# Ranking the last five steps by their whole chain, and issuing seven of eight stores from GpSimd, in a two-problem attention kernel

## The chip, the cores and the metric

The kernel runs on one core of a Trainium2 chip. The metric is the device time of one execution in microseconds (us), as the median of several runs; lower is better. A profiled execution gives the trace that all rows come from. Its engines are PE (matrix multiply; PEld is its weight load), DVE or VectorE, ACT or ScalarE, POOL or GpSimd, and SP or SyncE, which issues DMA transfers. "SPq" is SyncE's queue of DMA instructions.

## The reference

Two attention blocks over a key/value cache, A (grouped heads: 4 key/value heads for 32 query heads) and B (32 key/value heads), whose results are put side by side:

```python
def _B_ref(x, k_cache, v_cache, wq, wo):      # B, Sq, D = 16, 32, 1024; H, Sk, Dh = 32, 1024, 128
    q = (x @ wq).reshape(B, Sq, H, Dh).transpose(0, 2, 1, 3)
    scores = einsum("bhqd,bhkd->bhqk", q, k_cache) * Dh ** -0.5
    p = softmax(scores, axis=-1)
    o = einsum("bhqk,bhkd->bhqd", p, v_cache)
    return o.transpose(0, 2, 1, 3).reshape(B, Sq, H * Dh) @ wo
# _A_ref is the same with k and v of 4 heads, each repeated for 8 query heads
a = _A_ref(A_x, ...); b = _B_ref(B_x, ...)
return concatenate([a, b], axis=-1)           # 16 x 32 x 2048, bfloat16
```

All inputs are bfloat16. The caches of B alone are 2 x 128 MiB, so each byte is read once and used little.

## The kernel before, in words

The 512 token rows are handled in NG = 4 groups G of 128. Work is cut into quads: 128 B quads (two batches by two heads, each with 1024 keys) and 128 A quads (one batch, four query heads). Step t of the program holds B quad t and, a little ahead, an A quad; "B124" is B quad 124. The function `oproj(pi, blk, G)` multiplies what the quads of a group gave with a block of `wo`; "oA3.3" is A's last block (3) for group 3, "oB7.2" is B's last block (7) for group 2. Block by block the products are added in `acc`; after the last block the group's 128 x 1024 result is stored by one DMA of 256 KB. There are eight such stores, one for each of two problems and four groups.

One B quad goes through these operations, under the lines of the kernel before:

- two K transfers of 512 KB each (`kb_dma`, L772) into two of 8 K slots, and two V transfers of 512 KB each (`vb_dma`, L785) into one of 3 V slots. V of quad t can be issued when quad t - 3 has done its last use of the slot; K of quad t when quad t - 4 has done its scores. Transfers are issued in order by SyncE.
- a transpose of each K half on VectorE (`KBt_tr`, L806), scores on PE into one of two score buffers (`scoresB`, L847, 32 matmuls), the negated maximum on VectorE (`max`, L857), the exponential with its sum on ScalarE (`exp`, L870).
- a transpose of the probabilities on PE (`PT_tr`, L882), its copy out of PSUM (`PT_ev`, L531, by ScalarE or VectorE), the product with V on PE (`PVB`, L912; `PVA`, L904 for A), reciprocal (L921) and normalization (`norm`, L928 or L929), a small transpose (`OT_tr`, L934) and its copy (`OT_ev`, L531).
- after the last quad of a group the projection on PE (L703, two halves of 512 columns), for the last block two sums on VectorE (`accF`, L717), and the store (`out_dma`, L720).

PE's work other than scores goes through four PSUM banks that these operations take and free.

The order on every engine is made by a planner, `list_schedule`, when the program is built. It walks through the operations with assumed durations, and of those that could start within 0.35 us of the earliest it takes the one of highest rank `bl`. The rank is the length of the chain that hangs on an operation, but only through users of the same step or an earlier one (`STEP_NEAR = 0`), less 3 us for each step (`STEP_US`), so that earlier steps go first. What comes out is fixed: each engine runs its list in order and waits by semaphores. A wait of SyncE for an `accF` ahead of a store therefore also holds the transfers listed behind that store. At the end SyncE waits for every transfer's semaphore (L418).

Of the kernel before, what the change touches and what calls it, by code (L numbers as in the profile page):

```python
# [10 lines left out]
BF = mybir.dt.bfloat16  # L11
# [19 lines left out]
LOOK = 0.35  # L31
STEP_US = 3
STEP_NEAR = 0
QB0 = [0, 3, 6, 9]
QA0 = [13 + (i * 9) // 8 for i in range(8)]
QB1 = [24 + (i * 9) // 8 for i in range(8)]
# [25 lines left out]
def dma_time(op):  # L62
    size, us = PACKET.get(op.name, PACKET_DEFAULT)
    return op.dur / size * us / 16
# [48 lines left out]
class Prog:  # L113
# [118 lines left out]
    def list_schedule(self, lat=0.05, look=LOOK):  # L232
        ops = self.ops
        n = len(ops)
        users = [[] for _ in range(n)]
# [6 lines left out]
        def odur(op):  # L242
            if op.dma_key is not None:
                return DMA_FIRST + dma_time(op) + DMA_LAST
            return op.dur[0] + op.dur[1]
        bl = [0.0] * n
        for i in range(n - 1, -1, -1):
            m = 0.0
            for u in users[i]:
                v = bl[u] + lat  # L250
                if v > m and ops[u].step <= ops[i].step + STEP_NEAR:
                    m = v
            bl[i] = odur(ops[i]) + m + ops[i].prio + PRIO_BONUS.get(ops[i].name.split("@")[0], 0.0)
        for i in range(n):
            bl[i] -= STEP_US * ops[i].step
        ready_t = [0.0] * n
        free = {}
        ready = {}
# [182 lines left out]
def build(nc, pa, pb, out):  # L441
    P = 128
    Bn, Sq, D = pa["x"].shape
    NTOK = Bn * Sq
    assert Sq == 32 and Bn % 4 == 0
    NG = NTOK // P
# [21 lines left out]
    out_flat = out.rearrange("b s c -> (b s) c")  # L468
# [3 lines left out]
    cols = [0, D]  # L472

    pr = Prog()
    stack = contextlib.ExitStack()
    with stack:
        def sb(name, shape, dt):
            return stack.enter_context(nc.sbuf_tensor(name, shape, dt))
# [15 lines left out]
        acc = sb("acc", [P, 2, NG, D], F32)  # L494
# [14 lines left out]
        def bank(v):  # L509
            return ps_g[:, v.idx, :]  # L510
# [12 lines left out]
        def evac(dst_ap, src_ap, reads, writes, name, eng=None, wtag=None, rtag=None, mul=None):  # L523
            def emit(e):
                dst = dst_ap() if callable(dst_ap) else dst_ap
                src = src_ap() if callable(src_ap) else src_ap
                if mul is not None:
                    if hasattr(e, "activation"):
                        return e.activation(dst, src, ACTF.Copy, scale=mul)
                    return e.tensor_scalar(dst, src, mul, None, ALU.mult)  # L530
                return e.copy(dst, src) if hasattr(e, "activation") else e.tensor_copy(dst, src)  # L531
            eng = eng or "any"
            pr.add(eng, emit, reads=reads, writes=writes, name=name if eng == "any" else name + "@" + eng, wtag=wtag, rtag=rtag)
# [35 lines left out]
        def lazy_flush(prefix):  # L569
            last = -1  # L570
            for i, (k, _, _) in enumerate(lazy):
                if k[:len(prefix)] == prefix:
                    last = i
            for _ in range(last + 1):
                lazy.pop(0)[1]()
# [113 lines left out]
        def oproj(pi, blk, G):  # L689
            gp = (blk * NG + G) % 2  # L690
            nh = HS if pi == 0 else MS
            nblk = NSB if pi == 0 else NMSB
            OT = OTA_sb if pi == 0 else OTB_sb
            wo_ = woA_sb if pi == 0 else woB_sb
            wo_res = "woA" if pi == 0 else "woB"
            lazy_flush(("wo", pi, blk))
            for oh in range(NOH):
                v = Virt("bank", "pj")
                for h0_ in range(0, nh, 2):
                    def e_op(e, oh=oh, h0_=h0_, v=v):  # L700
                        last = None
                        for hh in range(h0_, h0_ + 2):
                            last = e.matmul(bank(v)[:, 0:OUTW], OT[:, gp, hh, :], wo_[:, hh, oh * OUTW:(oh + 1) * OUTW],  # L703
                                            start=(hh == 0), stop=(hh == nh - 1))
                        return last
                    pr.add("pe", e_op, reads=[("OT", pi, gp, h0_), ("OT", pi, gp, h0_ + 1), (wo_res, h0_), (wo_res, h0_ + 1)], writes=[v],
                           name="oprojA" if pi == 0 else "oprojB",
                           dur=0.45 * OUTW / 512, rtag={(wo_res, h0_): blk, (wo_res, h0_ + 1): blk, ("OTv", pi, gp): (blk, G)})
                a_ap = acc[:, pi, G, oh * OUTW:(oh + 1) * OUTW]
                o_ap = acc[:, pi, G, :].bitcast(BF)[:, oh * OUTW:(oh + 1) * OUTW]  # L710
                if blk == 0:
                    evac(a_ap, lambda v=v: bank(v)[:, 0:OUTW], reads=[], writes=[v, ("acc", pi, G, oh)], name="acc0")
                elif blk < nblk - 1:
                    pr.add("dve", lambda e, a_ap=a_ap, v=v: e.tensor_tensor(a_ap, a_ap, bank(v)[:, 0:OUTW], ALU.add),  # L714
                           reads=[], writes=[v, ("acc", pi, G, oh)], name="acc+")
                else:
                    pr.add("dve", lambda e, a_ap=a_ap, o_ap=o_ap, v=v: e.tensor_tensor(o_ap, a_ap, bank(v)[:, 0:OUTW], ALU.add),  # L717
                           reads=[], writes=[v] + [("acc", pi, G, x) for x in range(oh + 1)], name="accF")
            if blk == nblk - 1:
                pr.add("sp", lambda e: e.dma_start(out_flat[G * P:(G + 1) * P, cols[pi]:cols[pi] + D], acc[:, pi, G, :].bitcast(BF)[:, 0:D]),  # L720
                       reads=[("acc", pi, G, x) for x in range(NOH)], dma_key=f"out{pi}_{G}", name="out_dma", dur=P * D * 2)

        class Quad:
# [320 lines left out]
        def plan(t, f, *a):  # L1044
            q_plan.setdefault(t, []).append(lambda: f(*a))

        PER = 8 * NG
        for G in range(NG):
            plan(QB0[G], qprojB, 1, G)
        for p_ in range(NIT // PER - 1):  # L1050
            at = QB0[-1] if p_ == 0 else (p_ - 1) * PER + (QB1 if p_ == 1 else QB_T)[-1]
            plan(at, wq_load, 0, p_ + 1)
# [13 lines left out]
        def stepA(qA):  # L1066
            tA = qA.t % (NG * 8)
            if qA.t == min(1, NIT - 1):
                for hh in pro_heads:
                    qprojA_head(0, hh)  # L1070
                wo_loadA(0)
            quadA_all(qA)
            if qA.last_of_group:
                oproj(0, qA.s, qA.G)
                if qA.G == NG - 1 and qA.s + 1 < NSB:
                    wo_loadA(qA.s + 1)

        for t in range(NIT):
            cur_step[0] = t
            pr.step = t  # L1080
            qB = quadsB[t]
            tB = t % (NG * 4)
            quadB_all(qB)
            target = min(NIT, -(-(t + 1) * NIT // NAS))
            while ia[0] < target:
                stepA(quadsA[ia[0]])
                ia[0] += 1
            tn = t + (4 - t % 4)
            if tn < NIT:
                qn = quadsB[tn]  # L1090
                if t % 4 == 0:
                    qprepB_tr(qn.m, qn.G)
                    qprepB_sh(qn.m, qn.G)
            for what in q_plan.get(t, ()):
                what()
            if qB.last_of_group:
                oproj(1, qB.m, qB.G)
                if qB.G == NG - 1 and qB.m + 1 < NMSB:
                    wo_loadB(qB.m + 1)
            lazy_pop(LAZY_PER_STEP)  # L1100
# [3 lines left out]
        if SCHED:  # L1104
            pr = pr.list_schedule()
# [41 lines left out]
```

## Time and profile before

| what | value |
|---|---|
| median of 3 runs | 891.7 us (891.68 to 892.2) |
| profiled execution | 894.39 us, of it the span 892.3 us |
| granted PE clock, mean | 0.994 |
| HBM read / written | 337.64 MB / 2.10 MB, 381 GB/s over the span |
| PE, VectorE, ScalarE busy | 92%, 83%, 68% of the span |
| POOL busy | 1.1 us, 8 instructions |
| stores (`out_dram`) | 8 of 256 KB, issued by SyncE, median 8.0 us from issue to landing |

The span runs from the first instruction to the last of the profiled execution; 2.09 us of that execution lie outside it. A row of a window gives the busy time and the number of instructions for each engine. A row of the chain gives its start, its length and what ran. A row of the timeline gives start, length, engine, line and operation. The time from issue to landing of a transfer contains its wait behind others in the queue.

### The profile page before, as it was taken

What the parts mean: (1) busy time and instruction counts of PE and PEld (TensorE: products, weight loads), DVE (VectorE), ACT (ScalarE), POOL (GpSimd) and SP (SyncE); (2) the same over time, 40 slices, a digit from 0 to 9 for tenths busy, and PEclk for the clock granted to TensorE, in tenths of its full rate; (3) what the DMA queues carried; (4) which work ended last, traced back from release to release, by engine and by line L of the source; (5) the groups of instructions that cost most, each with busy time, mean ns of one, the idle gap of its engine ahead of it and who ended that gap; (6) DMA issues with size and microseconds to landing.
All of it is one profiled execution on the core that took longest, in us unless ns stands there. A gap on an engine that the chain in (4) does not pass through costs nothing.

```text
span 892.3 us, 29320 instructions
## 1 busy us (share of the span) xinstructions
PE 820.2 (92%) x12864; PEld 469.4 (53%) x12864; DVE 739.5 (83%) x1030; ACT 608.6 (68%) x1347; POOL 1.1 (0%) x8
## 2 busy tenths in 40 slices
PE   6999899999999999999999999999899878978976
PEld 3365565556555455555555555555456545544543
DVE  0398888879987888889898888898899889888985
ACT  3387886776768577675777677676767767565763
POOL 0000000000000000000000000000000000000000
PEclk9999999999999999999999999999999999998999
DMA  9999999999999999999999999999999999999994
GB/s 318 397 395 392 391 393 396 392 389 395 395 366 387 396 395 390 380 393 395 395 393 394 391 393 394 372 395 394 394 378 380 393 395 395 396 394 382 394 374 166
DMA packets 145278, 341.65 MB, mean 383 GB/s; under 512 B 12032, under 2 KB 12032, under 8 KB 145152
## 3 DMA queue, kind: packets, MB, share of 16 engines
q1 hardware_dynamic: 145152, 339.79, 100.7%
q8 instruction: 101, 1.65, 0.8%
q14 instruction: 25, 0.20, 0.1%
HBM read 337.64 MB, written 2.10 MB: 381 GB/s over the span
## 4 chain that ended last, share of the span: by engine, by line
PE 53%; DMA 18%; DVE 14%; ACT 9%; SPq 3%; issue 1%; DVEq 0%; ACTq 0%
DMA KB_sb<-in_B_k_cache_dram 14%; PE ps_s L847 12%; PE ps_g L703 9%; PE ps_g L882 9%; ACT P_sb L870 6%; DVE stat L857 6%; DVE KB_sb L806 6%; PE ps_g L912 5%; PE ps_g L615 4%; PE ps_g L904 4%; PE ps_s L827 3%; PE ps_g L634 3%; PE ps_g L798 2%; ACT PT_sb L531 2%; SPq L785 2%; DMA VB_sb<-in_B_v_cache_dram 1%
## 5 line engine op out<-in xcount | busy, mean ns | idle before, releaser
L857 DVE TENSOR_REDUCE stat<-ps_s 128x1 f32<-128x1024 f32 x256 | 305.4, 1208 | 53.3 <-PE ps_s L847 43.9
L806 DVE STREAM_TRANSPOSE KB_sb<-KB_sb 128x1024 f32<-128x1024 f32 x256 | 310.2, 1230 | 35.8 <-DMA KB_sb<-in_B_k_cache_dram 32.7
L870 ACT ACTIVATE P_sb<-ps_s,stat 128x1024 bf16<-128x1024 f32 x256 | 286.1, 1119 | 60.9 <-DVE stat L857 59.2
L882 PE MATMUL ps_g<-id,P_sb 128*128 128x128 f32 x1024 | 172.7, 295 | 9.7 <-ACT OTA_sb L531 3.2
L847 PE MATMUL ps_s<-KB_sb,QR 32*32 32x512 bf16 x4096 | 160.1, 397 | 23.1 <-ACT P_sb L870 17.4
L882 PEld LDWEIGHTS ps_g<-id,P_sb 128*128 128x128 f32 x1024 | 149.1, 207 | 48.1 <-issue 9.2
L531 ACT COPY PT_sb<-ps_g 128x512 f32<-128x512 f32 x238 | 138.2, 593 | 50.9 <-PE ps_g L882 49.8
L928 ACT ACTIVATE O_sb<-ps_g,stat 128x128 bf16<-128x128 f32 x186 | 67.9, 371 | 62.9 <-PE ps_g L912 36.5
L912 PE MATMUL ps_g<-VB_sb,PT_sb 128*32 128x128 bf16 x4096 | 92.0, 224 | 7.0 <-ACT PT_sb L531 3.6
L847 PEld LDWEIGHTS ps_s<-KB_sb,QR 32*32 32x32 bf16 x4096 | 47.1, 89 | 85.0 <-ACT P_sb L870 27.0
L827 PE MATMUL ps_s<-KTA_sb,QT_sb 128*128 128x512 bf16 x256 | 87.0, 383 | 4.2 <-ACT P_sb L870 4.1
L912 PEld LDWEIGHTS ps_g<-VB_sb,PT_sb 128*32 128x32 bf16 x4096 | 60.5, 97 | 55.3 <-issue 36.4
L904 PE MATMUL ps_g<-VA_sb,PT_sb 128*128 128x128 bf16 x1024 | 77.6, 220 | 3.1 <-ACT PT_sb L531 1.2
L904 PEld LDWEIGHTS ps_g<-VA_sb,PT_sb 128*128 128x128 bf16 x1024 | 61.0, 98 | 31.6 <-issue 13.9
L634 PE MATMUL ps_g<-wq_sb,xT_sb 128*128 128x512 bf16 x256 | 72.8, 388 | 3.9 <-DMA wq_sb<-in_B_wq_dram 3.9
L703 PE MATMUL ps_g<-woB_sb,OTB_sb 128*128 128x512 bf16 x256 | 67.6, 380 | 3.4 <-ACT PT_sb L531 1.3
L703 PE MATMUL ps_g<-woA_sb,OTA_sb 128*128 128x512 bf16 x256 | 62.5, 380 | 0.8 <-DVE OTA_sb L531 0.3
L934 PE MATMUL ps_g<-ident,O_sb 128*128 128x128 bf16 x256 | 52.5, 223 | 4.5 <-ACT O_sb L928 3.6
L615 PE MATMUL ps_g<-xT_sb,wq_sb 128*128 128x512 bf16 x192 | 55.5, 380 | 0.4 <-ACT QR L531 0.2
L870 ACT ACTIVATION_READ_ACCUMULATOR P_sb<-ps_s,stat 128x1 f32 x256 | 51.6, 202 | 0.0
L531 ACT COPY OTA_sb<-ps_g 128x64 f32<-128x64 f32 x114 | 24.5, 216 | 37.2 <-PE ps_g L934 36.6
L714 DVE TENSOR_TENSOR acc<-acc,ps_g 128x512 f32<-128x512 f32 x64 | 41.0, 675 | 8.7 <-PE ps_g L703 8.4
(42 smaller groups left out, 511.9 us busy)
## 6 DMA issues: line engine op xcount, KB each, us to landing
VB_sb<-in_B_v_cache_dram SPq DMA_DIRECT2D x256, 512.0 KB, 12.2
KB_sb<-in_B_k_cache_dram SPq DMA_DIRECT2D x256, 512.0 KB, 12.4
KA_sb<-in_A_k_cache_dram SPq DMA_DIRECT2D x64, 256.0 KB, 12.3
VA_sb<-in_A_v_cache_dram SPq DMA_DIRECT2D x64, 256.0 KB, 12.2
wq_sb<-in_B_wq_dram SPq DMA_DIRECT2D x16, 512.0 KB, 10.5
woB_sb<-in_B_wo_dram SPq DMA_DIRECT2D x32, 256.0 KB, 11.3
woA_sb<-in_A_wo_dram SPq DMA_DIRECT2D x32, 256.0 KB, 9.9
wq_sb<-in_A_wq_dram SPq DMA_DIRECT2D x12, 512.0 KB, 11.3
```

The costliest lines, as they stand in the source:

```text
L531: return e.copy(dst, src) if hasattr(e, "activation") else e.tensor_copy(dst, src)
L615: last = e.matmul(bank(v)[:, 0:tn], w_[:, j, hh * Dh:(hh + 1) * Dh], xT_sb[:, 0, j, t0:t0 + tn], start=(j == 0), stop=(j == DJ - 1))
L634: last = e.matmul(bank(v)[:, 0:CW], xT_sb[:, 1, j, G * P:(G + 1) * P], wq_sb[:, j, mh * CW:(mh + 1) * CW], start=(j == 0), stop=(j == DJ - 1))
L703: last = e.matmul(bank(v)[:, 0:OUTW], OT[:, gp, hh, :], wo_[:, hh, oh * OUTW:(oh + 1) * OUTW], start=(hh == 0), stop=(hh == nh - 1))
L806: pr.add("dve", lambda e: e.transpose(KB_sb[:, sl, :].bitcast(F32), KB_sb[:, sl, :].bitcast(F32)), writes=[("KB", sl)], name="KBt_tr", rta ...
L827: pr.add("pe", lambda e, u=u: e.matmul(ps_s[:, vS.idx, u, :], qt[:, q.b, q.hh0:q.hh0 + 4, :].rearrange("p a q -> p (a q)"), KTA_sb[:, sl, ...
L847: last = e.matmul(ps_s[32 * cg:32 * cg + 32, vS.idx, g2, :].rearrange("p (s j) -> p s j", s=16), lhsT, rhs, start=(fp == 0), stop=(fp == 3 ...
L857: pr.add("dve", lambda e: e.tensor_reduce(stat[:, vst.idx, 0:1], ps_s[:, vS.idx, :, :], AXIS.XY, ALU.max, negate=True), writes=vS.res + [v ...
L870: return e.activation(dst, src, ACTF.Exp, bias=stat[:, vst.idx, 0:1], scale=1.0, accum_out=stat[:, vst.idx, 1:2])
L882: last = e.transpose(bank(vb)[:, m * P:(m + 1) * P], p32[:, m:Sk // 2:NPK], id32[:])
L904: last = e.matmul(bank(vb)[:, 0:Dh], ptc_of(vPT, c, 0, P), VA_sb[:, kvs, c, :], start=(c == 0), stop=(c == NCH - 1))
L912: last = e.matmul(bank(vb)[32 * a:32 * a + 32, 0:Dh], ptc_of(vPT, c, 32 * a, 32 * a + 32), VB_sb[:, kvs, a // 2, a % 2, c, :], start=(c == ...
```

## The change

The planner computes a second length, `full`, for each operation: the whole chain behind it through users of all steps, to the end of the program. For operations of steps 123 to 127 (`TAIL_STEP = 123`; there are 128 steps) this length, set against the longest among them and raised by 12, takes the place of the rank, and the deduction per step stops growing at step 123. Ranks of earlier steps stay as they were. In `oproj`, the store of the result is issued by GpSimd, except the last one (B, group 3), which stays with SyncE. All else is as before: the same operations, buffers, slots and semaphores. Lines move down by 3 at the top of the file and by 9 from L258 on, so that L720 becomes L729.

```diff
+TAIL_STEP = 123
+TAIL_GAIN = 1.0
+TAIL_BASE = 12.0
...
             bl[i] = odur(ops[i]) + m + ops[i].prio + PRIO_BONUS.get(ops[i].name.split("@")[0], 0.0)
+        full = [0.0] * n
+        for i in range(n - 1, -1, -1):
+            full[i] = odur(ops[i]) + max((full[u] + lat for u in users[i]), default=0.0)
+        base = max((full[i] for i in range(n) if ops[i].step >= TAIL_STEP and ops[i].dma_key is None), default=0.0)
         for i in range(n):
-            bl[i] -= STEP_US * ops[i].step
+            if ops[i].step >= TAIL_STEP:
+                bl[i] = TAIL_GAIN * (full[i] - base) + TAIL_BASE
+            bl[i] -= STEP_US * min(ops[i].step, TAIL_STEP)
...
             if blk == nblk - 1:
-                pr.add("sp", lambda e: e.dma_start(out_flat[...], acc[...]),
+                pr.add("sp" if pi == 1 and G == NG - 1 else "pool", lambda e: e.dma_start(out_flat[...], acc[...]),
                        reads=[("acc", pi, G, x) for x in range(NOH)], dma_key=f"out{pi}_{G}", name="out_dma", dur=P * D * 2)
```

The order of the four engine lists differs from before in two stretches: a short one where the first stores of the result stood in SyncE's list, and the last one from step 123 on. The number of instructions is the same on PE, VectorE and ScalarE together.

## The prediction

> **What bounds the kernel now.** I read the page first, then the windows of the last 30 us, the chain, and the queues of SyncE and VectorE. "B124" is the B quad of step 124, and V127 or K127 the two V or K transfers of quad B127; counting instructions in the kernel's order gives each row its quad.
>
> The page:
> ```profile
> span 892.3 us, 29320 instructions
> ...
> DMA  9999999999999999999999999999999999999994
> ```
> All 16 DMA engines are busy up to the last slice, at some 395 GB/s (the GB/s row): up to about 864 us the kernel waits for bytes, and an order of instructions can win only behind that. The last stretches (PE, PEld, DVE, ACT, POOL busy, clock, DMA share, GB/s):
> ```profile
> 856.00:864.00 8.00, 5.65 (x84) 3.92 (x84) 6.98 (x12) 4.94 (x11) 0.00 (x0) 0.87 1.04 400
> 864.00:868.00 4.00, 4.00 (x91) 2.24 (x98) 2.09 (x3) 1.70 (x6) 0.00 (x0) 0.83 0.79 306
> ...
> 872.00:876.00 4.00, 3.33 (x36) 1.89 (x38) 3.90 (x6) 0.59 (x1) 0.00 (x0) 1.00 0.84 308
> 876.00:880.00 4.00, 2.30 (x85) 1.01 (x81) 3.75 (x6) 1.55 (x4) 0.00 (x0) 1.00 0.63 179
> 880.00:884.00 4.00, 3.71 (x100) 2.54 (x83) 2.40 (x5) 3.26 (x7) 0.00 (x0) 1.00 0.45 171
> ```
> From 864 on no single resource is full: DMA fades while the engines wait for one another. The chain there (start, us, what):
> ```profile
> 868.50 1.88 PE ps_g L703 x8
> ...
> 870.41 0.69 DVE acc L717
> 871.10 3.41 DVE KB_sb L806 x3
> 874.51 0.58 DVE acc L717
> ...
> 875.87 0.57 DVE KB_sb L806
> ...
> 876.95 1.19 DVE stat L857
> ...
> 885.01 0.63 PE ps_g L912 x32
> ```
> Projections and their sums (L703, L717) stand between the last key transposes (L806) and the next maximum (L857). The second K half of B126 landed at 869.44, yet its transpose ran only at 875.79 because VectorE's order put both sums of A's last projection ahead of it. The maximum of B125 (scores ready at 871.03) started at 876.95, and all later softmaxes followed. The landings themselves are even: K127 at 870.75 and 872.06, V125 and V126 at 873.40, 874.70, 876.08 and 877.40, one 512 KB transfer per 1.31 us. Then SyncE's queue has nothing to send:
> ```profile
> 866.99 1.92 SPq L785 DMA_DIRECT2D VB_sb<-in_B_v_cache_dram  x4
> 871.13 0.36 SPq L720 DMA_DIRECT2D out_dram<-acc  x1
> 876.41 0.88 SPq L785 DMA_DIRECT2D VB_sb<-in_B_v_cache_dram  x2
> 877.34 11.88 SPq L720 DMA_DIRECT2D out_dram<-acc  x2
> ```
> V127 needs the V slot of B124, whose PVB ends at 876.36. So V127 is issued at 876.41 and lands at 880.75 and 882.09. That is still not the last thing: PVB of B127 starts at 885.01, 2.9 us after its V. Behind it come 7.29 us to the end of the span (885.01 to 892.30): PVB, normalization, transpose, half the projection, two sums of 0.69, the store's issue at 888.86, 2.1 us to landing, 1.4 us of final waits.
>
> **Part 1, the ranking of steps 123 to 127.** It adds and removes no instruction; it reorders. In the program of the changed kernel the tail reads as follows. PE: PVB122, PVA126, scores B124, PVB123, half of A's last projection, scores B125, PVB124; the remaining projection pieces go in between the scores of B126 and B127. VectorE: four key transposes without a sum between them, maxima of B126 and B127, and only then the sums of oA3.3 and oB7.2.
>
> First, the transfers. PVB122 no longer stands behind PVB123, which waited until 861.90 for V123. PT of B122 ended at 858.29, so PVB122 can run near 860 instead of ending at 866.94. PVB123 keeps its place (V123 lands at 861.65). V124 landed at 866.90, and PVB124 now precedes A's second half projection. About 868.5 instead of 876.36 follows from 866.90 plus the rows ahead of it (scores 0.9, PVA 0.6). V127 is then issued about 868.6, while V125 and V126 still stream until 877.40. It follows them without a hole: 877.40 + 2 x 1.31 = 880.0. It can't be earlier, as the landings are already back to back.
>
> Second, the arithmetic from K127's landing at 872.06. Key transpose 1.23: 873.3. Maximum of B126: 874.5; scores of B127 take 1.14 beside it; maximum of B127 1.2: 875.7. Reciprocals and one normalization 0.7, first sum 0.7: 877.1, which frees the bank for PT of B126; the second sum frees the one of B127 at 877.8. PT 0.63, PT evacuations on ScalarE 0.59 each: 879.0. PVB126, normalization and transpose of O: 879.8. PE must do from 862.3 on what it did from 861.9 to 885.0, less PVB122 and PVA126. By starts back to back: scores 4 x 0.9, PVB 4 x 0.46, PT 5 x 0.47, PVA 0.47, projections 12 x 0.435, small transposes 0.5, together 14.0 us in 17.9 us. So arithmetic is ready at about 879.8 and V127 at 880.0: the two meet and V127 decides by a hair.
>
> PVB127 starts 0.25 after landing (the row 861.65 to 861.90): 880.25. With the unchanged 7.29 behind it the span is 887.54, a gain of 4.8. I take off 0.3 for oA3.3's store, whose 0.64 (877.40 to 878.03, the store there before) can fall into V127's stream, and 0.3 for waits of 0.02 to 0.05 at the more numerous switches of PE. Gain: 4.2.
>
> **Part 2, stores by GpSimd.** Seven issues of 0.36 us leave SyncE's queue, and with them its waits for the sums: 23.4 us in six waits in the view of waits, the longest (11.0) with no load behind it. Nothing is queued on POOL behind a waiting store but other stores, and nobody on chip reads the result. Until 864 this hides behind the DMA queue, which holds 12 us of transfers (12.2 us from issue to landing) against waits of 1.6 to 3.5 us there: worth 0. If that cover were gone, at most the dip of 812 to 820 us (355 and 365 GB/s for 395) comes back, 0.7 us. The planner no longer charges SyncE for stores, so PE's order also changes between about 755 and 790 us; with 390 to 406 GB/s there, 0.
>
> No row shows a store issued by POOL. Bounds: 0.62 us of stream for 256 KB as in the row of oB7.1 (landings of the K transfer ahead of it and of itself, 852.41 and 853.03), or the whole 2.07 us of the one store that met an empty queue (888.86 to 890.92), as if nothing flowed beside it. A gain is excluded, as the bytes are the same. I take 0.62, the row of a store in a full stream, and keep 1.45 extra per store for a rival. At the end the store of oB7.2 is ready at about 880.4 and must land by SyncE's last landing, about 886.2: 5.8 us for 2.07.
>
> VectorE is busy 3.90 of 4.00 us in 872 to 876, with f32 transposes of 1.23 us. [...]
>
> **The sum.** 892.30 - 4.2 = 888.1 us of span. The profiled execution took 894.39 (2.09 around the span), 2.7 more than the median of 891.7. I take the difference over to the median: 891.7 - 4.2 = **887.5 us**.
>
> **Rivals.**
> 1. The arithmetic becomes the bound by PE's clock. The trace grants 0.50 from 862 to 865 after PE idled, which here would cost some 1.7 us of PE work (half of 3.4). For it: PE idles wherever it outruns K. Against: 3.9 us of slack, and 1.00 from 868 on. Time 887.5 + 1.7 = 889.2.
> 2. The projections moved late cost as much as they did early. PT of B126 waits for a bank that a sum frees, so if the sums come later than worked out, everything behind stands still. For it: four banks shared by four projection halves and the quads. It takes 3.9 + 0.3 of delay to cancel the gain: 891.7.
> 3. GpSimd's last store ends last. If GpSimd could issue only once VectorE is through with its last sum (about 884.0), two stores one after the other at 2.07 each land at 888.1, 1.9 after SyncE's last store; some 1.0 of SyncE's 1.4 of final waits runs meanwhile, so the end moves by 0.9: 888.4. [...]
> 4. Slower: stores outside SyncE's queue interrupt the loads. Six of them start before V127 has landed; at 1.45 extra each that is 8.7, so 896.2. From 1.0 extra each on ((4.2 + 1.8) / 6) the kernel is slower. For it: the stream is full, so nothing hides such a loss. Against: it is the same 16 engines and the same 128 rows of 2 KB.
>
> The program itself shows that the order changes as described, so a change without effect on the order is out.
>
> **Chances.** Forecast 0.58; rival 1 0.18; rival 2 0.10; rival 3 0.05; rival 4 0.09. About 0.2% (1.8 us) is what a measurement of this kernel can tell from no change. Faster takes the forecast, rival 3 and most of rival 1: 0.77. Same takes rival 2 and the rest of rival 1: 0.13. Slower: 0.10. The range starts at 886.0 (the full 4.8, the dip's 0.7, and 0.2 for a median's spread) and ends at 891.2, which leaves out rival 4 and half of rival 2.
>
> **What would show it.** In the changed profile the last V issue should stand near 868 to 870 and its landing near 880; L806 should run four times without L717 in between; the chain should pass through DMA VB_sb or the maxima of B126 and B127 shortly before a PVB at about 880 to 881; about 7.3 us should follow. The landings up to K127 should be at 872 +- 0.7. I am wrong if K127 lands later than 874 (stores cost stream), if PVB127 starts over 1 us after V127's landing (arithmetic), or if the final wait of SyncE is for a store by POOL.

## The result, and the profile after

The changed kernel takes 889.07 us (median of 7 runs, 887.83 to 889.90) against 892.13 us for the kernel before (median of 7). The medians lie 3.1 us apart, where 4.2 us had been forecast. The measured ratio is 0.9959, with a 95% interval of 0.9948 to 0.9969, so the kernel is faster by 0.31 to 0.52%. Two later groups of runs gave ratios of 0.9954 (0.9943 to 0.9966) and 0.9945 (0.9932 to 0.9959) for the same kernel, with medians 3.8 and 4.7 us apart. In what follows a gain in us is a difference of medians, and the ratios with their intervals say how sure it is.

The profiled execution took 889.07 us, of it 887.3 the span. Lines moved: L806 is now L815, L717 L726, L857 L866, L703 L712, L912 L921, L785 L794, and L720 L729. The page:

```profile
span 887.3 us, 29315 instructions
...
DMA  8999999999999999999999999999999999999995
...
q0 software_dynamic: 560, 1.84, 0.5%
...
out_dram<-acc POOLq DMA_DIRECT2D x7, 256.0 KB, 6.3
```

The DMA engines are full up to the last slice, as before. Queue q0 is new: it carries GpSimd's seven stores, which land 6.3 us after their issue in the median (8.0 before). The windows of the tail (PE, PEld, DVE, ACT, POOL busy, clock, DMA share, GB/s):

```profile
856.00:864.00 8.00, 6.92 (x138) 4.66 (x130) 7.20 (x10) 5.84 (x17) 0.00 (x0) 1.00 1.03 398
864.00:868.00 4.00, 3.61 (x52) 1.87 (x49) 2.66 (x4) 2.13 (x6) 0.00 (x0) 1.00 1.03 396
...
872.00:876.00 4.00, 4.00 (x89) 1.56 (x74) 3.15 (x4) 1.21 (x2) 0.00 (x0) 1.00 0.69 261
876.00:880.00 4.00, 3.47 (x52) 1.93 (x50) 2.41 (x9) 2.75 (x6) 0.54 (x1) 1.00 0.28 102
880.00:884.00 4.00, 2.67 (x42) 1.03 (x41) 1.99 (x3) 0.80 (x3) 0.54 (x1) 1.00 0.27 103
```

DMA holds its 396 GB/s through 868 us, where the kernel before had fallen to 306: the hole in the stream is gone, and the last V lands 2.0 us earlier after the last K. VectorE's timeline has the order that the forecast described, four key transposes (L815) without a sum (L726) between them and then the maxima (L866) of B126 and B127:

```profile
868.22 4.62 DVE L815 STREAM_TRANSPOSE KB_sb<-KB_sb 128x1024 f32<-128x1024 f32 x4
872.76 1.19 DVE L866 TENSOR_REDUCE stat<-ps_s 128x1 f32<-128x1024 f32 x1
874.80 1.22 DVE L866 TENSOR_REDUCE stat<-ps_s 128x1 f32<-128x1024 f32 x1 [0.85 <-PE ps_s L856]
```

SyncE's and GpSimd's timelines (start, length, what; in brackets what GpSimd idled for):

```profile
860.28 9.48 SPq L794 DMA_DIRECT2D VB_sb<-in_B_v_cache_dram  x6
883.78 0.36 SPq L729 DMA_DIRECT2D out_dram<-acc  x1
```

```profile
878.63 0.54 POOL L729 DMA_DIRECT2D out_dram<-acc  x1 [36.08 <-DVE acc L726]
880.91 0.54 POOL L729 DMA_DIRECT2D out_dram<-acc  x1 [1.74 <-DVE acc L726]
```

V127 is issued at 868.88 (876.41 before) and lands at 877.24 and 878.57. The stores of oA3.3 and oB7.2 land at 880.92 and 883.19, ahead of SyncE's last, issued at 883.78 and landed at 885.85. The chain of the tail (start, length, what):

```profile
873.67 1.11 PE ps_s L856 x28
...
874.80 1.11 DVE stat L866
...
876.48 0.60 DVE acc L726
...
877.13 1.23 PE ps_g L891 x8
...
879.89 0.17 PE ps_g L943
880.06 0.56 PE ps_g L921 x32
```

It runs through the maximum of B127 (L866), a first sum of the projection (L726) that frees a bank, both PT (L891), and PVB of B127 (L921 at 879.99). No row of it is a transfer: PVB of B127 started 1.42 us after its V had landed. There the chain differs from the forecast, which had V127 decide by a hair.

This table sets the runs below against the landing of the last K transfer, K127, since up to there the kernels wait for bytes. Times are from each run's trace, in us. The last column gives where, from 840 to 886 us, the clock granted in windows of 2 us was under 0.97. Each row is a single execution; those of the ranking only, of V127 held back and without V127 are the slowest of their five, 1.1 to 1.9 us over the median.

| kernel | K127 lands | V127 lands, after K127 | PVB of B127 starts, after K127 | last store lands | span | slow clock |
|---|---|---|---|---|---|---|
| before | 872.06 | 10.03 | 12.95 | 890.92 | 892.3 | 862 to 866 |
| changed | 870.52 | 8.05 | 9.47 | 885.85 | 887.3 | 848 to 854 |
| ranking only | 870.90 | 9.54 | 11.65 | 888.44 | 889.9 | 862 to 868 |
| stores only | 873.33 | 7.25 | 7.38 | 887.17 | 888.6 | none |
| changed, 2nd profile | 870.98 | 8.02 | 9.07 | 885.91 | 887.3 | 848 to 854 |
| V127 held back | 870.14 | 11.86 | 12.00 | 887.99 | 889.4 | 848 to 854, 870 to 874 |
| queue only | 871.60 | 9.77 | 12.91 | 890.44 | 891.8 | 860 to 866 |
| order only | 870.58 | 8.02 | 8.15 | 884.57 | 886.0 | 884 to 886 |
| without V127 | 871.52 | none | 10.45 | 887.83 | 889.2 | 850 to 854, 870 to 874 |
| three moves | 870.68 | 8.02 | 8.80 | 885.77 | 886.2 | 848 to 854 |
| PE kept busy | 870.49 | 8.01 | 8.14 | 884.50 | 885.9 | none |
| moves and busy | 869.97 | 9.51 | 9.72 | 885.97 | 886.4 | 868 to 872, 884 to 886 |
| changed, 3rd profile | 870.50 | 9.04 | 9.18 | 885.54 | 886.9 | 884 to 886 |

Of the 5.0 us between the spans of before and after, 1.5 stand at K127 already, and they stand at the first steps too: the second K half of B1 landed at 37.40 and at 35.87. With the order of before unchanged, the queue-only run has it at 35.80, so this is a difference between executions. From K127's landing to the end it is 20.24 before and 16.78 after: 3.5 us from the tail, close to the 3.1 of the medians.

### The profile page after: what moved, and what is told of

Its sections match the earlier page's. It is cut to its first block, busy times and chain, and to the rows that moved or that the text cites. A ratio compares the mean times of both kernels' runs of the same rounds, so it can differ in the third digit from the quotient of the medians.

```text
span 887.3 us, 29315 instructions
## 1 busy us (share of the span) xinstructions
PE 817.8 (92%) x12864; PEld 468.8 (53%) x12864; DVE 737.1 (83%) x1027; ACT 609.4 (69%) x1350; POOL 5.1 (1%) x15
## 4 chain that ended last, share of the span: by engine, by line
PE 56%; DMA 19%; DVE 10%; ACT 8%; SPq 4%; issue 1%; ACTq 0%; DVEq 0%
DMA KB_sb<-in_B_k_cache_dram 16%; PE ps_s L856 12%; PE ps_g L891 9%; PE ps_g L712 8%; ACT P_sb L879 5%; PE ps_g L921 5%; PE ps_g L624 5%; DVE stat L866 5%; DVE KB_sb L815 4%; PE ps_g L643 4%; PE ps_g L913 4%; PE ps_s L836 4%; PE ps_g L807 2%; SPq L794 2%; PE ps_g L943 1%; ACT PT_sb L540 1%
## 5 line engine op out<-in xcount | busy, mean ns | idle before, releaser
L866 DVE TENSOR_REDUCE stat<-ps_s 128x1 f32<-128x1024 f32 x256 | 305.6, 1208 | 53.9 <-PE ps_s L856 44.5
L815 DVE STREAM_TRANSPOSE KB_sb<-KB_sb 128x1024 f32<-128x1024 f32 x256 | 309.4, 1229 | 36.6 <-DMA KB_sb<-in_B_k_cache_dram 34.4
L891 PE MATMUL ps_g<-id,P_sb 128*128 128x128 f32 x1024 | 172.9, 296 | 10.8 <-ACT OTA_sb L540 3.8
L891 PEld LDWEIGHTS ps_g<-id,P_sb 128*128 128x128 f32 x1024 | 148.8, 207 | 49.4 <-issue 8.3
L921 PE MATMUL ps_g<-VB_sb,PT_sb 128*32 128x128 bf16 x4096 | 90.7, 222 | 4.6 <-ACT PT_sb L540 2.2
L921 PEld LDWEIGHTS ps_g<-VB_sb,PT_sb 128*32 128x32 bf16 x4096 | 59.8, 97 | 52.9 <-issue 36.8
L712 PE MATMUL ps_g<-woB_sb,OTB_sb 128*128 128x512 bf16 x256 | 68.1, 380 | 2.7 <-ACT PT_sb L540 1.3
L712 PE MATMUL ps_g<-woA_sb,OTA_sb 128*128 128x512 bf16 x256 | 63.0, 380 | 1.2 <-DVE OTA_sb L540 0.6
```

The lines of the kernel that those rows point to most:

```text
L815: pr.add("dve", lambda e: e.transpose(KB_sb[:, sl, :].bitcast(F32), KB_sb[:, sl, :].bitcast(F32)), writes=[("KB", sl)], name="KBt_tr", rta ...
L866: pr.add("dve", lambda e: e.tensor_reduce(stat[:, vst.idx, 0:1], ps_s[:, vS.idx, :, :], AXIS.XY, ALU.max, negate=True), writes=vS.res + [v ...
L891: last = e.transpose(bank(vb)[:, m * P:(m + 1) * P], p32[:, m:Sk // 2:NPK], id32[:])
L921: last = e.matmul(bank(vb)[32 * a:32 * a + 32, 0:Dh], ptc_of(vPT, c, 32 * a, 32 * a + 32), VB_sb[:, kvs, a // 2, a % 2, c, :], start=(c == ...
```

## The experiments

**First group: which half brings the gain?** Theory "order": the ranking. Theory "stores": a SyncE queue without stores. Theory "stores cost": GpSimd's stores hurt, and the ranking brings more than was seen.

Ranking only, all stores on SyncE:

```diff
-pr.add("sp" if pi == 1 and G == NG - 1 else "pool", lambda e: e.dma_start(out_flat[...], acc[...]),
+pr.add("sp", lambda e: e.dma_start(out_flat[...], acc[...]),
```

> The ranking alone; all eight stores issued by SyncE as before. Theory 'order' (the ranking brings the whole gain, in the tail, and who issues the stores is worth nothing): about 889.1, 3.1 us under the kernel before, with PVB of B127 some 9.5 us after K127's landing and 7.3 us from there to the end. Theory 'stores' (a queue of SyncE without stores brings a share of at least 1 us, by earlier issues of loads): 890.1 or more. Theory 'stores cost' (stores by GpSimd interrupt the stream, and the ranking brings more than was seen): 888 or less.

Measured: 889.71 us against 892.88, ratio 0.9966 (0.9954 to 0.9977): 3.2 us. The time lies between "order" (889.1) and "stores" (890.1) and can't tell them apart. The profile fits neither: PVB of B124 ended at 872.48 (868.84 in the changed kernel), V127 was issued at 872.53, and PVB of B127 came 11.65 after K127 and not 9.5. V127 did not hold it, as it landed 2.1 us earlier; the chain there runs through PE and VectorE, behind the slow stretch of the clock at 863.31 to 866.73.

Stores only, without the ranking (the changed line of `oproj` put into the kernel before):

> Seven stores issued by GpSimd, no ranking of the last steps. Theory 'order': no difference from the kernel before that can be measured (892.1, within 0.9), PVB of B127 again about 14 us after K127's landing. Theory 'stores': 889 to 891. Theory 'stores cost': 893 or more.

Measured: 890.21 us, ratio 0.9970 (0.9958 to 0.9981): 2.7 us. My theory fell here: the half that I had valued at nothing gains nearly as much as the other. Its chain:

```profile
873.25 7.32 DMA VB_sb<-in_B_v_cache_dram
880.58 0.14 issue
880.71 0.65 PE ps_g L912 x32
```

The chain goes through V127, and the arithmetic was ready at 879.92, ahead of it. The trace shows an order on the engines quite unlike that of before: all four sums of oA3.3 and oB7.2 are over at 870.25, ahead of the last three key transposes, and the maximum of B125 starts at 871.32 where it was 876.95. Each half by itself makes the planner lay out another tail: the ranking by intent, the stores because the planner no longer charges SyncE for them. (That SyncE's charge is the reason is read from the edit, which changes nothing else.) What this run can't tell is whether the gain comes from that order or from the free queue.

The changed kernel itself, as the measure:

> The changed kernel itself, as the measure for the others of this group: 889.1, 3.1 us (0.3 to 0.5%) under the kernel before by every theory.

Measured: 889.07 us, ratio 0.9954 (0.9943 to 0.9966), so 3.8 us. Two halves of 3.2 and 2.7 don't add up to it; they overlap.

V127 held back. The order on every engine is that of the changed kernel; V127 reads a mark that PVB of B125 writes:

```diff
+        pv = [k for k in seq if ops[order[k]].name == "PVB" and ops[order[k]].step == 125][-1]
+        late = [k for k in seq if ops[order[k]].name == "vb_dma" and ops[order[k]].step == 125]
+        seq = [k for k in seq if k not in late]
+        seq[seq.index(pv) + 1:seq.index(pv) + 1] = late
...
+            more = (("late",),)
+            newp.add(eng, emit, actual(reads) + more * (k in late), actual(writes) + more * (k == pv), ...)
```

> The changed kernel, same order on every engine, but the two V transfers of B127 wait until PVB of B125 has ended (875.8 in the changed kernel's profile), about when the kernel before issued them (876.41). Theory 'both parts are needed': issue at about 875.9, landings at about 880.2 and 881.6 (by 876.41 to 880.75 and 882.09 of before), PVB of B127 at 881.8 for 879.99, so 1.8 us over the changed kernel, about 890.9. Theory 'arithmetic alone' (the early issue of V127 brought nothing): 889.1, no difference from the changed kernel.

Measured: 890.13 us, ratio 0.9965 (0.9954 to 0.9977); 1.1 us over the changed kernel, a difference that the two intervals don't separate. The trace (L799 issues V127 here, and L926 is PVB, as each edit moves the lines a little):

```profile
876.82 0.37 SPq L799
877.19 0.04 issue
877.23 4.77 DMA VB_sb<-in_B_v_cache_dram
882.00 0.14 issue
882.14 0.63 PE ps_g L926 x32
```

PVB of B127 stands right behind V127, at 882.14 for 881.8 expected, 2.1 later than in the group's changed kernel (880.05), and the span of this profile is 2.1 longer. So a late V127 becomes the bound. How much of the gain the early issue brings is not shown. By the medians 2.75 of the 3.8 us are left without it, and the hold was harder than the wait of the kernel before: V127 was issued 6.68 us after K127's landing here and 4.35 us after it there.

**Second group: order or queue?** Now the planning and the issue are taken apart. Queue only: the program of before is planned with all stores on SyncE, and the engine is changed afterwards.

```diff
             eng, emit, reads, writes, dma_key, name, dur, tag, prio = self.specs[order[k]]
+            if name == "out_dma" and dma_key != "out1_3":
+                eng = "pool"
```

> The order that the kernel before has on every engine, instruction for instruction; only the issue of seven stores goes to GpSimd, after the planning. After the last group the theories are: 'order' (each half of the change gains by the other order that the planner gives the last 30 us; the queue that issues the stores is worth nothing) and 'queue' (what the stores-only kernel gained, 2.7 us, comes from SyncE's queue being free of stores). Order: as the kernel before, within 0.9 us, PVB of B127 about 13 us after K127's landing, as before (12.95). Queue: 2 to 3 us under it.

Measured: 892.47 us against 892.66, ratio 0.9995 (0.9986 to 1.0004). PVB of B127 came 12.91 after K127 (12.95 before). By the interval the queue brings something between a gain of 1.2 us and a loss of 0.4 us, so nothing that can be measured.

Order only: the changed kernel's order, and the same lines with `eng = "sp"` for all stores.

> The order of the changed kernel on every engine, instruction for instruction; only the issue of the seven stores goes back to SyncE, after the planning. Order: as the changed kernel, 3 to 4 us under the kernel before, PVB of B127 about 9.3 us after K127's landing. Queue: 1 us or more slower than the changed kernel, some 888 to 889 being missed by that much against the same runs of the kernel before.

Measured: 887.89 us, ratio 0.9944 (0.9931 to 0.9957), all of the gain. With the run before it this settles the question as far as the medians go, to about 1 us: the effect is the order that the planner writes. For the stores-only kernel it is inferred, as its order was not run with the stores on SyncE. In this profile the chain goes as the forecast had it:

```profile
867.62 10.97 DMA VB_sb<-in_B_v_cache_dram
878.60 0.14 issue
878.73 0.63 PE ps_g L923 x31
```

V127 decides, and PVB of B127 (L923) starts 8.15 after K127; 8.19 had been worked out. PE had idled 0.35 us ahead of it, so the arithmetic was ready 7.80 after K127, where the forecast had 7.74. So why 9.47 in the changed kernel's profile, with the same order? Two more runs of this group asked for it. In the first, V127 is not loaded at all (the order is kept):

```diff
+            if name == "vb_dma" and ops[order[k]].step == 125:
+                continue
```

> The changed kernel, its order kept, without the two V transfers of B127: PVB of B127 uses what its V slot held before, so that quad's output is not the reference's. 'Arithmetic' (in the changed kernel PVB of B127, 1.4 us after V127's landing, waits for the engines and not for V127): same time as the changed kernel within 0.6, PVB of B127 at K127's landing + 9.2 to 9.6. 'Transfer': PVB of B127 earlier by 1 us or more, and the time with it.

Measured: 889.30 us, ratio 0.9963 (0.9949 to 0.9977), no faster than the changed kernel in the other groups (0.9954 and 0.9945), which was not run in this one. In this execution PVB of B127 was even later (10.45), and two slow stretches of the clock lie ahead of it. "Transfer" is out for an execution of that kind.

In the second, three moves in the order, and the waits for the stores put last (`at` finds an operation by name and step, `ahead` moves it in front of another):

```diff
+        ahead(at("accF", TAIL_STEP, 0), at("max", 127))
+        ahead(at("PT_trB", 126), at("OT_tr", 125))
+        for j in range(4):
+            ahead(at("PVB", 127, j), at("OT_tr", 126))
...
-        final_waits = [... sorted(self.dma_count.items())]
+        final_waits = [... sorted(self.dma_count.items(), key=lambda x: (x[0].startswith("out"), x[0]))]
```

> The changed kernel with three moves in its order and one in its last waits: the first sum of oA3.3 goes ahead of the maximum of B127, into VectorE's gap of 0.85 us (873.95 to 874.80); PT of B126 goes ahead of the transpose of O of B125 on PE; PVB of B127 goes ahead of the transpose of O of B126; SyncE's last waits have those for the stores at their end instead of in the middle. 'Arithmetic': PVB of B127 0.3 to 1.1 us earlier against K127's landing, with V127's landing + 0.25 as the next limit, and 0.3 to 0.8 of that at the end; the time from the last store's landing to the end falls from 1.45 to about 0.5. Together 1.0 to 1.8 us under the changed kernel. 'Transfer decides, and the waits do not': no difference from the changed kernel.

Measured: 888.03 us, ratio 0.9948 (0.9935 to 0.9961). In the trace it does what was expected: PVB of B127 at 8.80 after K127, 0.3 to 0.7 less than in the two profiles of the changed kernel with the same slow stretch, and 0.43 from the last landing to the end (1.45). The medians don't show it: the order-only run of the same group, without these moves, took 887.89.

**Third group: the clock, and the price of a store.** The table's last column suggested a cause for the later arithmetic. The windows of the changed kernel around 850 us (clock in the third column from the right):

```profile
848.00:850.00 2.00, 0.90 (x24) 0.38 (x32) 1.73 (x6) 2.00 (x4) 0.00 (x0) 0.72 1.02 400
850.00:852.00 2.00, 2.00 (x29) 0.69 (x14) 1.89 (x2) 0.49 (x4) 0.00 (x0) 0.50 1.05 391
852.00:854.00 2.00, 1.81 (x42) 1.51 (x40) 2.00 (x3) 1.23 (x4) 0.00 (x0) 0.92 1.05 399
```

The deficits add up to 2 x (0.28 + 0.50 + 0.08) = 1.72 us of full clock, or 3.4 us at half of it. PE had worked 1.7 of the 4.2 us ahead (844.94 to 849.11). To keep it busy there, PVA of A124 is computed three times over:

```diff
-                    for c in range(NCH):
+                    for c in list(range(NCH)) * (3 if q.t == 124 else 1):
```

> The changed kernel, its order kept; PVA of A124 computes the same eight matmuls three times over (each time from the start, so the value is the same), which keeps PE busy for 1.24 us of the 1.46 that it idles at 847.64 to 849.11 in the changed kernel's profile, just ahead of the stretch 849 to 853 where the granted clock is 0.50 to 0.92. Theory 'clock' (the 1.3 us by which the arithmetic came later than worked out is that stretch, and it follows from PE's idling): no such stretch after 848, PVB of B127 at K127's landing + 8.1 to 8.4 (with no stretch the order-only run had 8.15), some 1.1 us under the changed kernel, 887.9. Theory 'the order itself' (sums and banks make the 1.3 us): PVB of B127 at K127's landing + 9.2 to 9.6 as before, 889.1, or later by what the repeated matmuls take.

Measured: 888.40 us, ratio 0.9945 (0.9931 to 0.9958). The repeats took 0.9 us and not 1.24 (PVA from 846.42 to 847.94 for 0.62). The windows:

```profile
848.00:850.00 2.00, 1.49 (x36) 0.62 (x37) 1.45 (x7) 1.58 (x4) 0.00 (x0) 1.00 1.03 406
850.00:852.00 2.00, 1.80 (x44) 1.55 (x41) 2.00 (x3) 1.40 (x4) 0.00 (x0) 1.00 1.03 385
852.00:854.00 2.00, 1.27 (x44) 0.88 (x40) 2.00 (x3) 1.46 (x3) 0.00 (x0) 1.00 1.06 401
```

No slow stretch, and PVB of B127 at 8.14 after K127, 0.13 behind V127, as "clock" has it. But the time is not measurably under that of the changed kernel in the same group (888.79, ratio 0.9945), whose own profile has no such stretch either. With everything together:

> The kernel with three moves in the order and the stores' last waits at the end, and with PVA of A124 computed three times over. 'Clock': PVB of B127 at V127's landing + 0.25 (K127's landing + 8.3), so 0.3 to 0.5 under what the moves alone gave, and the last store's landing 0.4 us before the end; 1.5 to 2.4 us under the changed kernel, 886.7 to 887.6. 'The order itself': as with the moves alone, about 888.0.

Measured: 888.31 us, ratio 0.9942 (0.9930 to 0.9955). Nothing more: the stretch at 849 is absent again, but one stands at 868 to 872 (0.67 and 0.50), and V127 landed 9.51 after K127. There is no version here that beats the changed kernel measurably.

The changed kernel once more:

> The changed kernel once more, as the measure for this group and for how often the slow stretch of the clock stands at 849 to 853: 889.1 and, as in five profiles of this order out of six, a stretch there, PVB of B127 at K127's landing + 9.0 to 9.5.

Measured: 888.79 us, ratio 0.9945 (0.9932 to 0.9959), and an execution without the slow stretch at 849, of the very same program. Its chain:

```profile
868.06 11.48 DMA VB_sb<-in_B_v_cache_dram
879.54 0.14 issue
879.68 0.63 PE ps_g L921 x32
```

Here V127 decides, as forecast. The scores of B127 ended 3.0 us after K127's landing, against 4.2 and 3.8 in the two profiles with the stretch. V127's second half landed 2.45 us after the first and not 1.33, with GpSimd's store of oA3.3, issued at 877.39, in between.

Last, 20 more stores by GpSimd in the full stream:

```diff
+            if pi == 1 and 2 <= blk <= 6:
+                pr.add("pool", lambda e: e.dma_start(scratch[...], acc[:, pi, G, 0:D // 2]),
+                       reads=[("acc", pi, G, x) for x in range(NOH)], dma_key=f"sc_{G}", ...)
```

> The changed kernel with 20 more stores of 256 KB issued by GpSimd, half of the accumulators of B after its blocks 2 to 6 to a place of their own in memory, in the full stream between about 270 and 800 us. Theory 'bytes' (a store by GpSimd costs the stream its bytes' time, 0.62 to 0.66 us each): 12 to 14 us over the changed kernel, 901 to 903. Theory 'interrupts' (1.45 extra each, the rival of the prediction): 41 us over it, 930. If reading and writing overlapped somewhere: less than 10 us.

Measured: 901.45 us, 12.7 over the changed kernel of the same group, or 0.63 us for each store of 256 KB. That is "bytes"; "interrupts" is out by a factor of three. The planner gave this program another order from 256 us on as well, but the trace has 11.7 us of the difference at K127's landing already (882.16 for 870.50), up to where both kernels wait for bytes.

```profile
scratch<-acc POOLq DMA_DIRECT2D x20, 256.0 KB, 6.2
```

## Why the prediction was right, and where it was not

The direction and, in the main, the mechanism held: a new order in the last 30 us, through V127 and the arithmetic behind K127. The time missed by 1.6 us, 1.1 of it in the gain and 0.4 in the base (892.13 for 891.7), and 889.07 is nearer to rival 1's 889.2 than to the forecast. That the profiled span of 887.3 stands so near the 888.1 worked out is partly luck. K127 landed 1.5 us earlier than in the profile before and outside the 872 +- 0.7 that was given as a sign; from K127 to the end 16.0 us were forecast and 16.8 measured.

**The transfers** came as worked out. V127 was issued at 868.88 (868.6 forecast) behind a stream without a hole, and landed 8.05 after K127 (880.0 - 872.06 = 7.94 forecast). Held back, it was the bound again.

**The arithmetic** was the mis-sized term. By the forecast's own test (PVB of B127 over 1 us behind V127) it was wrong in the profile shown: 9.47 after K127 for 8.19. In the order-only and PE-kept-busy profiles the same steps in the same order gave 8.15 and 8.14. The step that failed is the one on PE's clock: I counted a slow stretch only where the trace of before had one, at 862 to 865, with slack behind it, and full clock elsewhere. In five of seven profiles that keep PE's order of the changed kernel through that stretch, without repeats, the stretch stands at 849 to 854, where no slack is left. It costs up to 1.7 us of PE work, and between profiles of one and the same program the scores of B127 ended 0.8 to 1.2 us later with it. This is rival 1's mechanism, at its price, in another place. With the idle time filled it was absent in two of two profiles, and without filling in two of seven, too few to show that PE's idling brings it on; the last section counts PE's work over all traces and shows the link.

The wait for a bank, rival 2's, was in the sum and came: in the changed kernel's profile PT of B126 (877.13) waited for the first sum (to 877.08), its exponential having ended at 875.10. The sum ended 6.56 us after K127 for 5.04 forecast. With PE kept busy the same wait stands there, but the sum ended at 4.87 after K127 and V127 decided. So the bank lies on the chain only where the scores are late: there the three moves, which put that sum earlier, brought PVB of B127 forward by 0.3 to 0.7 us.

**Behind PVB of B127** 7.29 us were forecast; it took 7.3.

**The stores.** The queue's worth of 0 holds (0.9995, 0.9986 to 1.0004). What I wrote of the planner doesn't: I saw that without SyncE's stores it orders PE differently between 755 and 790 us, put that at 0, and credited the tail to the ranking alone. It changes the tail as well, for 2.7 us by itself. The sum didn't suffer, since I had read the tail from the changed program as a whole; the split between the parts did. The 0.62 us for a store was right (0.63). The 0.3 taken off for oA3.3's store stands between 0 in the profile shown (V127 landed ahead of the store's issue) and 1.1 in the third.

**Rival 3** did not come: GpSimd issued its last store 0.3 us after its sum, and it landed 2.66 us before SyncE's. That GpSimd could issue only once VectorE is through was an assumption, and the runs don't bear it out. In the changed kernel's profile each of the seven issues started 0.29 to 0.31 us after its sum; five ran beside a transpose or a maximum of VectorE and two beside none, and all took 0.54 us but the first (0.68). Of the 27 store issues in the run with 20 more, 24 ran while VectorE was busy for at least part of them, and all but the first took 0.54 us (that one 0.68).

**Rival 4** is out by the 0.63 us per store.

## What to carry to other kernels

Where a planner writes the order, an edit that only moves work to another queue is also an edit of the order; plan with one assignment and issue with the other to tell the two apart. Before crediting a gain to a part, run each part alone, and expect that two parts which each repair the same tail don't add up. Where the end of a kernel hangs on a chain with a few tenths of slack, read several profiles of one program: what decides may differ from one execution to the next, as here: PVB of B127 started 1.4 and 1.1 us behind the landing of V127 in two profiles of the changed kernel and 0.14 behind it in the third.

## What the runs showed of the hardware that was not expected

The slow stretches of PE's clock before 875 us last 3.41 us at 0.50 each (1.7 us lost; one, in the ranking-only run, lasts 6.83), and they stand partly in other places in each execution. Within a trace their starts lie whole multiples of 3.413 us apart, to within 1 ns in the first profiles of the kernels before and after, and to within 0.05 us in the other twelve traces by the granted clock in windows of 2 us; with V127 held back they are, from 800 us on, at 801.76, 808.59, 849.55 and 870.03. So the time can be cut into such windows of 3.413 us, and PE's busy time, as the profile has it, counted in each. Of 3409 windows at full clock between 30 and 875 us, 17 had PE busy for less than 1.56 us, and the next window was at half clock behind every one of them. Of the 133 with 1.56 to 2.3 us it was so behind 27, and behind none of the 3259 with more. The five windows ahead of the stretch at 849 had 1.12 to 1.55 us of work, and PE's longest idle time there, to the stretch's start or just past it, was 1.62 us with the three moves and 1.46 or 1.47 in the other four profiles that have the stretch. The same idle time gave no stretch where the windows fell otherwise (1.70 us in the order-only profile, 1.93 in the changed kernel's third), and with the repeats the windows there had at least 2.17 us. What decides between 1.56 and 2.3 us stays open.

The last V transfer landed 8.01 to 9.51 us after the last K in profiles that issue it behind the same four transfers. The longest came ahead of any store: in that run (moves and busy) V127's first half landed at 878.16, 2.84 us behind the transfer before it, and GpSimd's store was issued at 878.40. DMA moved 206 GB/s from 872 to 874 there, where the changed kernel's first profile has 326, and all transfers had long been issued. Its cause stays open.
